# Differences of the Fourier matrix blocks made in layer 1's prologue, beside the value products, and loaded by both Fourier layers

## The chip, the cores and the metric

The kernel runs on one core of one Trainium2 chip. The metric is the device time of one execution in microseconds (us), given as the median over runs. A core has a matrix engine (PE, with its weight loads shown as PEld), a vector engine (DVE), a scalar engine (ACT), a general engine (POOL), and SyncE (SP), whose queue issues nearly all transfers (DMA) here. In the text, layers are counted from 0.

## The reference

Four layers are applied to x of shape 2048 × 640 in float32: sliding-window attention, Fourier mixing, attention, Fourier mixing. Each is added to its input.

```python
def _A_ref(x, wqkv, wo):                       # layers 0 and 2
    H = 32; Dh = D // H; W = 256
    q, k, v = ...                              # x @ wqkv, split into 32 heads of 20
    scores = jnp.einsum("bhqd,bhkd->bhqk", q, k) * (Dh ** -0.5)
    mask = (idx[:, None] - idx[None, :] >= 0) & (idx[:, None] - idx[None, :] < W)
    p = _softmax(jnp.where(mask[None, None], scores, -1e9))
    return (p @ v) @ wo
def _B_ref(x, dft_seq_re, dft_seq_im, dft_hid_re, dft_hid_im):   # layers 1 and 3
    a = jnp.einsum("bsd,ed->bse", x, dft_hid_re)
    b = jnp.einsum("bsd,ed->bse", x, dft_hid_im)
    return jnp.einsum("ts,bse->bte", dft_seq_re, a) - jnp.einsum("ts,bse->bte", dft_seq_im, b)
x = x + _A_ref(_layernorm(x), ...)
x = x + _B_ref(_layernorm(x), ...)
```

and the last two lines once more.

## The kernel before

**Layers.** `network` calls `attention` for layers 0 and 2 and `fourier` for layers 1 and 3. The instructions of each engine run in the order in which the code writes them: the schedule is manual, and where functions are interleaved, a hand-written order with posted work and due times decides. Every product is made of three products of rounded halves: `split` (L223 on; its rows show as L226 on ACT and L232 on DVE) cuts an operand into a high and a low half.

**The Fourier layers' first pass.** The product with the sequence matrix is done in four passes (sb, part), each with eight blocks j of 128 rows. A fast-multiplication scheme with seven products uses, beside the matrix's own blocks, differences of them. The input `c` holds for every (sb, part, j) a row of four blocks of 512 columns, c0 to c3; the scheme needs c1 − c0 (kind 0, units "a1" and "a2"), c2 − c1 (kind 1, units "b", "b7", "b5") and c2 − (c1 − c0) (kind 2, unit "g"). Pass (0, 0) is special: it runs while the attention layer ahead of it is still finishing its last rows (`late`, with `staged` posted into it), so its products (L1415) stand among that layer's output products and hidden-dimension products (L239, L694). `load_to` issues the loads, `cut_to` makes the differences and splits them, `seq` issues the products.

In layer 1, `load_to` fetches 512 KB pieces of c (L1268), `cut_to` and `staged` make the 24 differences (L1287, L1324, L1335 and L1344, on DVE or POOL), and `keep` has each stored to a scratch tensor `c_d` in device memory (256 KB each, issued from `seq`). `sums_kept` is set at the end of the first Fourier layer. In layer 3, `load_to` then fetches the block itself and the stored difference in 256 KB pieces (L1254, L1264, L1266), and the subtractions are left out, but for L1346, which makes a further difference in both layers. The later passes make their differences themselves in both layers.

**The prologue of layer 0.** `before_heads` normalizes x, transposes it, multiplies it by the weights of q, k and v, and ends before the first head. Its tiles t = 0 to 15 have 128 rows each. `prep` loads one tile ahead (L318), takes its statistics on DVE (L286 to L290), normalizes it (L304) and turns it on PE (L341). `value(t)` (a value call) makes two products on PE of 128 × 320 for tile t, 15 matmuls each, in two PSUM banks out of three (5, 6, 7) that the role "v" takes in turn: six banks for three calls, so the first bank of a call is one that the second half of the call two before, or the first half of the one before, had. After the products comes `prep()`, and then the two halves are copied out of PSUM, the first by ACT, the second by DVE (L442). Every second call stores 768 KB of values to `v_d` (L444). Ahead of each of the calls 4 to 7, 8 to 11 and 12 to 15 stand `packed` steps, which issue 24, 12 and 12 transfers `kp<-qk_d` and `qp<-qk_d` of 80 KB (L594) on SP. Between them stand `pieces`, products for q and k (L239 too). After call 15 the first head's projection begins (L257); its banks are two of the same three.

SP issues in the order of the code. A transfer that has to wait for a semaphore (data to store, a buffer to be free) holds back what stands behind it in that queue.

**Buffers.** `pt` is four tiles of 128 × 1536. `pt[0]` and `pt[1]` stage the values in the prologue (in the rows: pt_95, pt_96). `pt[2]` and `pt[3]` (pt_97, pt_98) hold raw value weights at the very start and are then free until the heads.

Of the kernel before, what the change touches and what calls it, by code (L numbers as in the profile page):

```python
# [7 lines left out]
F32 = mybir.dt.float32  # L8
# [56 lines left out]
class Net:  # L65
    def __init__(self, nc, tc, ctx, a):
# [27 lines left out]
        self.rd = dram.tile([NSB, H, 512], F32, name="r_d")  # L94
        self.cd = dram.tile([3, NB // 2, P, 512], F32, name="c_d")
        self.sums_kept = False
        self.xs = [dram.tile([S, D], F32, name=f"x_d{i}") for i in range(3)]
# [270 lines left out]
    def before_heads(self, xsrc):  # L368
# [47 lines left out]
        def pieces(sb):  # L416
            for c in range(2):
# [4 lines left out]
                if ready or sb and state[0] < 4 * sb + 8:  # L422
                    prep()

        def value(t):
            v, xt = vst[t // 2 % 2], self.xnt(t // 4)
            rs = slice((t % 4) * P, (t % 4 + 1) * P)
            ps = []
            for hf in range(2):
# [4 lines left out]
                ps.append(p)  # L434
            prep()
            for hf in range(2):
                dst = v[:, 4 * hf:4 * hf + 4, t % 2, 0:84].rearrange("p q (h c) -> p q h c", c=21)[:, :, :, 1:21]
                src = ps[hf].rearrange("p (q h c) -> p q h c", q=4, h=4)
                if hf == 0:
                    nc.scalar.activation(dst, src, AF.Copy)  # L440
                else:
                    nc.vector.tensor_copy(dst, src)  # L442
# [43 lines left out]
        packed(3)  # L486
        values(3)
        self.ones_rows(1)

# [541 lines left out]
    def late(self, xsrc, xdst, hook):  # L1031
# [30 lines left out]
        for t in range(NB):  # L1062
# [32 lines left out]
            if t == NB - 2:  # L1095
                u = self.last_a2 - 1
                self.post(3, lambda u=u: self.staged(u, 0, nc.vector))
                self.post(6, lambda u=u: self.staged(u, 1))
                self.post(9, lambda u=u: self.staged(u, 2))
            hook(t)  # L1100
# [92 lines left out]
    def take_fourier(self):  # L1193
# [23 lines left out]
        self.acc = {}  # L1217
        self.leaving, self.keeping = [], []

# [28 lines left out]
    def load_to(self, n):  # L1248
        while self.n_load <= min(n, len(self.order) - 1):
# [3 lines left out]
            if ph == "a2" and self.kept_sum(u):  # L1253
                self.nc.sync.dma_start(self.t1[j], self.cd[0, j])  # L1254
            if ph in ("a2", "b5"):
# [17 lines left out]

    def keep(self, u, t):

        sb, part, ph, j = self.order[u]
        if not self.sums_kept and sb + part == 0:
            kind = {"a1": 0, "b": 1, "b7": 1, "g": 2}[ph]
            self.keeping.append(lambda: self.nc.sync.dma_start(self.cd[kind, j], t))

    def staged(self, u, stage, eng=None):
# [10 lines left out]
        self.split(c[0], c[1], (q, p)[stage - 1])  # L1292
        out.append(c)
        if stage == 1:
            self.kept[j] = c

    def cut_to(self, n):
        nc = self.nc
        while self.n_cut <= min(n, len(self.order) - 1):
# [5 lines left out]
            if ph == "b7":  # L1305
                if j:
                    self.staged(u, 0, nc.gpsimd)
                    self.staged(u, 1)
                    self.staged(u, 2)
                continue  # L1310
# [10 lines left out]
            if ph in ("a", "a1"):  # L1321
                eng = nc.vector if ph == "a1" else nc.gpsimd
                if not self.kept_sum(u):
                    eng.tensor_tensor(out=t1, in0=q, in1=p, op=OP.subtract)  # L1324
                    if ph == "a1":
                        self.keep(u, t1)
                src = [p] + ([t1] if ph == "a" else [])
# [5 lines left out]
            elif ph == "b":  # L1333
                if not self.kept_sum(u):
                    nc.vector.tensor_tensor(out=p, in0=q, in1=p, op=OP.subtract)  # L1335
                    self.keep(u, p)
                src = [q, p]
            else:
                cut(q)
                eng = nc.vector if self.order[u][:2] == (0, 0) and j < 3 else nc.gpsimd  # L1340
                if self.kept_sum(u):
                    t1, p = p, t1
                else:
                    eng.tensor_tensor(out=t1, in0=p, in1=t1, op=OP.subtract)  # L1344
                    self.keep(u, t1)
                nc.vector.tensor_tensor(out=p, in0=t1, in1=q, op=OP.subtract)  # L1346
# [227 lines left out]
    def fourier(self, xsrc, xdst, more):  # L1574
# [205 lines left out]
        for g in range(NB // 2):  # L1780
# [11 lines left out]
        self.ready, self.hid, self.sums_kept = 8, False, True  # L1792

# [71 lines left out]
```

## Time and profile before

| | |
|---|---|
| runs | 2188.59, 2188.83, 2190.87 us; median 2188.83 |
| profiled execution, its own time | 2191.25 us |
| its span, first to last instruction | 2189.5 us |
| mean granted PE clock | 0.996 |
| transfers | 398.40 MB, mean 182 GB/s |
| read from and written to device memory | 273.94 and 120.06 MB |
| value calls 4 to 7 in layer 0, on PE | 53.14 to 72.6 us |
| layer 1's first pass beside the attention tail | about 533 to 652 us |
| the same in layer 3 | about 1626 to 1733 us |

Times in the profile count from the first instruction. A row of a timeline has the start, the duration, the engine and line, the operation with its output and inputs, the number of instructions, and in brackets the idle time ahead of it on its engine with what released it. For SP (shown as SPq) the duration is the time from the first issue of a group to the end of its last, waits between them included. The sum of the busy times is far above the span, because engines work side by side; what counts is what the engine that ends last waits for. Three rows of the page's groups and issues belong to the parts that the change touches:

```profile
L1344 POOL TENSOR_TENSOR pt<-pt,pt 128x512 f32<-128x512 f32 x32 | 46.2, 1445 | 232.5 <-DMA pt<-c 146.0
L226 ACT ACTIVATE c<-pt 128x512 fp32r<-128x512 f32 x146 | 90.4, 625 | 108.2 <-POOL pt L1324 56.4
pt<-c SPq DMA_DIRECT2D x166, 512.0 KB
```

The columns of the first two are: busy us and mean ns of one, then the idle time of the engine ahead of the group and what ended it. The third is a group of transfers: loads of c, 166 of them, 512 KB at the median.

### The profile page before, as it was taken

What the parts mean: (1) busy time and instruction counts of PE and PEld (TensorE: products, weight loads), DVE (VectorE), ACT (ScalarE), POOL (GpSimd) and SP (SyncE); (2) the same over time, 40 slices, a digit from 0 to 9 for tenths busy, and PEclk for the clock granted to TensorE, in tenths of its full rate; (3) what the DMA queues carried; (4) which work ended last, traced back from release to release, by engine and by line L of the source; (5) the groups of instructions that cost most, each with busy time, mean ns of one, the idle gap of its engine ahead of it and who ended that gap; (6) DMA issues with size and microseconds to landing.
All of it is one profiled execution on the core that took longest, in us unless ns stands there. A gap on an engine that the chain in (4) does not pass through costs nothing.

```text
span 2189.5 us, 48923 instructions
## 1 busy us (share of the span) xinstructions
PE 2119.5 (97%) x17872; PEld 1785.8 (82%) x17872; DVE 1600.5 (73%) x3931; ACT 1139.8 (52%) x2125; POOL 958.5 (44%) x1562
## 2 busy tenths in 40 slices
PE   7999999898999999999999999998999999999999
PEld 7987777677878888889999877776778888888899
DVE  6358888786897868786661588887867968687766
ACT  3117777656554545452341277776566645455332
POOL 3037776765513232332330376767655023241324
PEclk9999999999999999999999999999999999999999
DMA  5546666785566454656646566667855454546653
GB/s 183 175 156 190 199 180 210 213 222 172 200 192 188 129 183 140 212 185 200 205 156 177 161 187 196 186 204 208 216 165 180 141 187 135 166 152 209 225 166 126
DMA packets 227088, 398.40 MB, mean 182 GB/s; under 512 B 39968, under 2 KB 86560, under 8 KB 226848
## 3 DMA queue, kind: packets, MB, share of 16 engines
q1 hardware_dynamic: 226848, 395.28, 57.8%
q8 instruction: 141, 2.31, 0.5%
q14 instruction: 99, 0.81, 0.1%
HBM read 273.94 MB, written 120.06 MB: 180 GB/s over the span
## 4 chain that ended last, share of the span: by engine, by line
PE 79%; DVE 6%; DMA 4%; ACT 4%; POOL 3%; issue 2%; SPq 1%; ACTq 0%; DVEq 0%; POOLq 0%
PE banks L1415 29%; PE banks L239 15%; PE banks L257 12%; PE banks L694 6%; PE banks L659 5%; PE banks L1703 5%; PE banks L631 5%; DVE banks L636 1%; DMA qp<-qk_d 1%; ACT pt L669 1%; DVE qp L232 1%; PE banks L341 1%; DMA qk_d<-c 1%; ACT big L1038 1%; SPq L594 1%
## 5 line engine op out<-in xcount | busy, mean ns | idle before, releaser
L636 DVE CUSTOM_DVE_ANT_0 banks<-banks,mask 128x384 f32<-128x384 f32 (+2 forms) x1024 | 527.1, 556 | 121.4 <-PE banks L631 98.6
L669 ACT ACTIVATE pt<-banks 128x768 f32<-128x768 f32 (+2 forms) x512 | 393.5, 771 | 170.7 <-PE banks L659 59.8
L675 POOL TENSOR_SCALAR_AFFINE_SELECT pt<-pt 128x256 f32<-128x256 f32 x512 | 213.8, 418 | 220.3 <-ACT pt L669 201.6
L257 PE MATMUL banks<-big,wc 64*128 64x512 f32 x1920 | 271.4, 394 | 0.4 <-DVE pt L442 0.4
L659 PE MATMUL banks<-qp,kp 61*128 61x384 f32 (+2 forms) x1024 | 211.4, 382 | 24.2 <-DVE mc L636 17.0
L631 PE MATMUL banks<-kp,qp 60*128 60x384 f32 (+2 forms) x1024 | 206.9, 348 | 8.8 <-DVE mc L636 8.5
L694 PE MATMUL banks<-pt,vq 128*32 128x128 f32 x5760 | 211.2, 278 | 3.5 <-ACT pt L669 3.5
L257 PEld LDWEIGHTS banks<-big,wc 64*128 64x128 f32 x1920 | 187.3, 186 | 22.2 <-ACT x L544 1.3
L679 POOL TENSOR_SCALAR_AFFINE_SELECT pt<-pt 128x256 f32<-128x256 f32 x448 | 193.8, 433 | 0.0
L226 ACT ACTIVATE qp<-pt 128x512 fp32r<-128x512 f32 (+1 forms) x200 | 123.1, 625 | 129.3 <-DVE pt L1346 50.2
L232 DVE TENSOR_TENSOR qp<-pt,qp 128x512 fp32r<-128x512 f32 (+1 forms) x198 | 156.3, 797 | 40.9 <-ACT qp L226 39.3
L694 PEld LDWEIGHTS banks<-pt,vq 128*32 128x32 f32 x5760 | 142.2, 110 | 51.5 <-issue 36.2
L659 PEld LDWEIGHTS banks<-qp,kp 61*128 61x128 f32 x1024 | 108.6, 185 | 88.8 <-DVE mc L636 65.8
L1415 PE MATMUL banks<-qp,big 128*128 128x512 f32 x648 | 153.6, 391 | 0.1
L631 PEld LDWEIGHTS banks<-kp,qp 60*128 60x128 f32 x1024 | 124.7, 187 | 33.7 <-DVE mc L636 21.8
L1344 POOL TENSOR_TENSOR pt<-pt,pt 128x512 f32<-128x512 f32 x32 | 46.2, 1445 | 232.5 <-DMA pt<-c 146.0
L226 ACT ACTIVATE c<-pt 128x512 fp32r<-128x512 f32 x146 | 90.4, 625 | 108.2 <-POOL pt L1324 56.4
L636 DVE DVE_READ_ACCUMULATOR2_ANT mc<- 128x1 f32 x1024 | 144.3, 141 | 0.0
L1415 PEld LDWEIGHTS banks<-qp,big 128*128 128x128 f32 x648 | 120.8, 188 | 24.9 <-POOL qp L232 0.9
L232 DVE TENSOR_TENSOR c<-pt,c 128x512 fp32r<-128x512 f32 x144 | 116.6, 813 | 26.7 <-ACT c L226 24.1
L1415 PE MATMUL banks<-qp,xc 128*128 128x512 f32 x480 | 118.2, 394 | 3.6 <-DVE xc L232 2.1
L552 POOL CAST c<-x 128x512 fp32r<-128x512 f32 x64 | 38.9, 611 | 166.5 <-ACT x L544 162.3
(253 smaller groups left out, 4477.0 us busy)
## 6 DMA issues: line engine op xcount, KB each, us to landing
pt<-c SPq DMA_DIRECT2D x166, 512.0 KB
qk_d<-c SPq DMA_DIRECT2D x80, 512.0 KB
kp<-qk_d SPq DMA_DIRECT2D x384, 80.0 KB
qp<-qk_d SPq DMA_DIRECT2D x384, 80.0 KB
kp<-u_d SPq DMA_DIRECT2D x32, 640.0 KB
o_d<-ou SPq DMA_DIRECT2D x64, 256.0 KB
x_d<-x SPq DMA_DIRECT2D x48, 320.0 KB
v_d<-pt SPq DMA_DIRECT2D x16, 768.0 KB
```

The costliest lines, as they stand in the source:

```text
L226: nc.scalar.activation(hi, src, AF.Copy, scale=-1.0 if neg else 1.0)
L232: (eng or nc.vector).tensor_tensor(out=lo, in0=src, in1=hi.bitcast(F32), op=OP.subtract)
L239: self.nc.tensor.matmul(p, x, y, start=n == 0, stop=n == last)
L257: self.nc.tensor.matmul(ps[a], x[r], y[r], start=half + i == 0, stop=half == 1 and i == n - 1, skip_group_check=True)
L631: nc.tensor.matmul(p, qp[quad % 2][b:b + 60, z, qb * P:(qb + 1) * P], kp[quad % 2][b:b + 60, z, k0 * P:(qb + 1) * P], start=True, stop=True)
L636: nc.vector.tensor_tensor_reduce(out=p, in0=p, in1=self.mask[:, 384 - n * P:], scale=1.0, scalar=NEG, op0=OP.add, op1=OP.max, accum_out=mc ...
L659: nc.tensor.matmul(self.banks[:, banks[e], :n * P], kp[quad % 2][b:b + 61, z, kb * P:(kb + 1) * P], qp[quad % 2][b:b + 61, z, kb * P:(kb + ...
L669: nc.scalar.activation(pt[quad, kb][:, 2 * z:2 * z + 2, :n * P], self.banks[:, b0:b1 + 1, :n * P], AF.Exp, scale=SCALE)
L675: nc.gpsimd.affine_select(out=t[:, :, 0:P], in_=t[:, :, 0:P], pattern=[[0, 2], [1, P]], compare_op=OP.is_ge, fill=0.0, base=0, channel_mul ...
L679: nc.gpsimd.affine_select(out=t[:, :, 256:384], in_=t[:, :, 256:384], pattern=[[0, 2], [-1, P]], compare_op=OP.is_gt, fill=0.0, base=0, ch ...
L694: nc.tensor.matmul(self.banks[32 * h:32 * h + 32, bank, :P], vq[:, 96 * (kb % 4) + 21 * h:96 * (kb % 4) + 21 * h + 32], t[:, h, (qb - kb) ...
L1415: nc.tensor.matmul(self.banks[:, bk, :], p, b[q], start=start and m == 0, stop=stop and last and m == 2, skip_group_check=True)
```

## The change

A new function `presum(n)` in `before_heads` makes all 24 differences of pass (0, 0), for layer 0 alone (`first`). For each j there are three stages, one per value call: load c0, c1 and c2 (768 KB) into `pt[2]` or `pt[3]`; subtract three times in place on DVE; store the 768 KB to `c_d`, which now has one row of 1536 columns per j. Even j use `pt[2]`, odd j `pt[3]`, one call later. It is called as `presum(t - 4)` in `value(t)`, after the products and `prep()` and ahead of the two copies out of PSUM, and once more after the last call, where it stores j = 7. So call 4 loads j = 0; call 5 subtracts j = 0 and loads j = 1; call 15 stores j = 6 and subtracts j = 7.

Both Fourier layers then load their differences: `kept_sum` is true for every unit of pass (0, 0). `keep`, `keeping` and `sums_kept` are gone, `staged` has lost its subtracting stage, and `posted` work for it at delay 3 too.

```diff
@@ before_heads
+        def presum(n):
+            for b in range(2):
+                j, stage = 2 * ((n - b) // 3) + b, (n - b) % 3
+                if not 0 <= j < NB // 2:
+                    continue
+                t = self.pt[2 + b]
+                c0, c1, c2 = cuts(t, 512)
+                if stage == 0:
+                    nc.sync.dma_start(t, a["c"][0, 0, j][:, :1536])
+                elif stage == 1:
+                    for out, x, y in ((c0, c1, c0), (c1, c2, c1), (c2, c2, c0)):
+                        nc.vector.tensor_tensor(out=out, in0=x, in1=y, op=OP.subtract)
+                else:
+                    nc.sync.dma_start(self.cd[j], t)
...
@@ value
             prep()
+            if first:
+                presum(t - 4)
             for hf in range(2):
...
@@ end of before_heads
         values(3)
+        if first:
+            presum(NB - 4)
...
@@ load_to
             if ph == "a2" and self.kept_sum(u):
-                self.nc.sync.dma_start(self.t1[j], self.cd[0, j])
+                self.nc.sync.dma_start(self.t1[j], self.cd[j, :, :512])
...
                 if ph != "a1":
-                    self.nc.sync.dma_start(p, self.cd[1 + (ph == "g"), j])
+                    at = 1024 if ph == "g" else 512
+                    self.nc.sync.dma_start(p, self.cd[j, :, at:at + 512])
...
     def kept_sum(self, u):
-        return self.sums_kept and self.order[u][:2] == (0, 0)
+        return self.order[u][:2] == (0, 0)
-
-    def keep(self, u, t):
...
@@ staged
-        if stage == 0:
-            if not self.kept_sum(u):
-                eng.tensor_tensor(out=p, in0=q, in1=p, op=OP.subtract)
-                self.keep(u, p)
-            return
...
@@ cut_to
             if ph in ("a", "a1"):
-                eng = nc.vector if ph == "a1" else nc.gpsimd
-                if not self.kept_sum(u):
-                    eng.tensor_tensor(out=t1, in0=q, in1=p, op=OP.subtract)
-                    if ph == "a1":
-                        self.keep(u, t1)
+                if ph == "a":
+                    nc.gpsimd.tensor_tensor(out=t1, in0=q, in1=p, op=OP.subtract)
...
@@ seq
-        for f in self.keeping:
-            f()
-        self.keeping.clear()
```

PE's instructions keep their order. What moves on SP and DVE stands in three places. The first is SP's queue in layer 0's prologue, from the packing before value call 4 to the stores of call 7. Before:

```order
L594 DMA kp_561<-qk_d 20x2x512 x6
L594 DMA qp_106<-qk_d 20x2x512 x6
L318 DMA x<-x 128x640 x2
L444 DMA v_d<-pt_95 128x8x192
L444 DMA v_d<-pt_96 128x8x192
L524 DMA qk_d<-c 128x2x512 x2
```

and with the change:

```order
L613 DMA kp_561<-qk_d 20x2x512 x6
L613 DMA qp_106<-qk_d 20x2x512 x6
L317 DMA x<-x 128x640
L433 DMA pt_97<-c 128x1536
L317 DMA x<-x 128x640
L433 DMA pt_98<-c 128x1536
L461 DMA v_d<-pt_95 128x8x192
L438 DMA c_d<-pt_97 128x1536
L433 DMA pt_97<-c 128x1536
L438 DMA c_d<-pt_98 128x1536
L461 DMA v_d<-pt_96 128x8x192
L543 DMA qk_d<-c 128x2x512 x2
```

Five transfers of 768 KB stand between the tiles of x and the value stores, the first load ahead of the second x tile.

The second place is DVE in the value calls 5 and 6 (a call's rows begin with the split of the turned tile, `big<-banks,big`, and the copies are L442 before and L459 after). Before:

```order
L232 TENSOR_TENSOR big_512<-banks,big_512 128x4x128
L232 TENSOR_TENSOR big_512<-banks,big_512 128x128
L442 COPY pt_95<-banks 128x4x4x20
L286 BN_STATS st<-x 128x6 x2
L288 BN_AGGR mv<-st 128x2
L290 TENSOR_SCALAR rs<-mv 128x1
L304 TENSOR_SCALAR x<-x,mv,rs 128x640
L232 TENSOR_TENSOR big_732<-banks,big_732 128x4x128
L232 TENSOR_TENSOR big_732<-banks,big_732 128x128
L442 COPY pt_96<-banks 128x4x4x20
```

and with the change:

```order
L231 TENSOR_TENSOR big_512<-banks,big_512 128x4x128
L231 TENSOR_TENSOR big_512<-banks,big_512 128x128
L436 TENSOR_TENSOR pt_97<-pt_97 128x512 x3
L459 COPY pt_95<-banks 128x4x4x20
L285 BN_STATS st<-x 128x6 x2
L287 BN_AGGR mv<-st 128x2
L289 TENSOR_SCALAR rs<-mv 128x1
L303 TENSOR_SCALAR x<-x,mv,rs 128x640
L231 TENSOR_TENSOR big_737<-banks,big_737 128x4x128
L231 TENSOR_TENSOR big_737<-banks,big_737 128x128
L436 TENSOR_TENSOR pt_98<-pt_98 128x512 x3
L459 COPY pt_96<-banks 128x4x4x20
```

Three subtractions stand ahead of each copy, behind the splits.

The third place is SP's queue around the value calls 12 to 15, from the packing before them to the first transfers for the heads. Before:

```order
L594 DMA qp_106<-qk_d 20x2x512 x6
L444 DMA v_d<-pt_95 128x8x192
L444 DMA v_d<-pt_96 128x8x192
L492 DMA kp_104<-ones 1x32x128 x2
L621 DMA vq_92<-v_d 128x384
L621 DMA vq_93<-v_d 128x384
```

and with the change:

```order
L613 DMA qp_106<-qk_d 20x2x512 x6
L438 DMA c_d<-pt_97 128x1536
L433 DMA pt_97<-c 128x1536
L438 DMA c_d<-pt_98 128x1536
L461 DMA v_d<-pt_95 128x8x192
L433 DMA pt_98<-c 128x1536
L438 DMA c_d<-pt_97 128x1536
L461 DMA v_d<-pt_96 128x8x192
L438 DMA c_d<-pt_98 128x1536
L511 DMA kp_104<-ones 1x32x128 x2
```

Each load of c into a buffer now stands right behind the store out of the same buffer, or two places behind it.

More of the change, by code (lines that the diff above doesn't have):

```diff
@@ L94, in __init__ @@
         self.rd = dram.tile([NSB, H, 512], F32, name="r_d")
-        self.cd = dram.tile([3, NB // 2, P, 512], F32, name="c_d")
-        self.sums_kept = False
+        self.cd = dram.tile([NB // 2, P, 1536], F32, name="c_d")
         self.xs = [dram.tile([S, D], F32, name=f"x_d{i}") for i in range(3)]
@@ L1096, in late @@
                 u = self.last_a2 - 1
-                self.post(3, lambda u=u: self.staged(u, 0, nc.vector))
-                self.post(6, lambda u=u: self.staged(u, 1))
-                self.post(9, lambda u=u: self.staged(u, 2))
+                self.post(6, lambda u=u: self.staged(u, 0))
+                self.post(9, lambda u=u: self.staged(u, 1))
             hook(t)
@@ L1217, in take_fourier @@
         self.acc = {}
-        self.leaving, self.keeping = [], []
+        self.leaving = []
     def take_rest(self):
@@ L1271, in kept_sum, with staged @@
     def kept_sum(self, u):
-        return self.sums_kept and self.order[u][:2] == (0, 0)
-    def keep(self, u, t):
[L1276 to L1281, printed above, removed]
+        return self.order[u][:2] == (0, 0)
+    def staged(self, u, stage):
         j, out = self.order[u][3], self.cut_of.setdefault(u, [])
         p, q = cuts(self.raw_of[u], 512)
-        if stage == 0:
-            if not self.kept_sum(u):
-                eng.tensor_tensor(out=p, in0=q, in1=p, op=OP.subtract)
-                self.keep(u, p)
-            return
         c = self.ring.popleft()
         self.ring.append(c)
-        self.split(c[0], c[1], (q, p)[stage - 1])
+        self.split(c[0], c[1], (q, p)[stage])
         out.append(c)
-        if stage == 1:
+        if stage == 0:
             self.kept[j] = c
@@ L1306, in cut_to @@
                 if j:
-                    self.staged(u, 0, nc.gpsimd)
+                    self.staged(u, 0)
                     self.staged(u, 1)
-                    self.staged(u, 2)
                 continue
@@ L1335, in cut_to @@
                     nc.vector.tensor_tensor(out=p, in0=q, in1=p, op=OP.subtract)
-                    self.keep(u, p)
                 src = [q, p]
@@ L1339, in cut_to @@
                 cut(q)
-                eng = nc.vector if self.order[u][:2] == (0, 0) and j < 3 else nc.gpsimd
                 if self.kept_sum(u):
@@ L1343, in cut_to @@
                 else:
-                    eng.tensor_tensor(out=t1, in0=p, in1=t1, op=OP.subtract)
-                    self.keep(u, t1)
+                    nc.gpsimd.tensor_tensor(out=t1, in0=p, in1=t1, op=OP.subtract)
                 nc.vector.tensor_tensor(out=p, in0=t1, in1=q, op=OP.subtract)
@@ L1791, in fourier @@
                     behind(at)
-        self.ready, self.hid, self.sums_kept = 8, False, True
+        self.ready, self.hid = 8, False
 def network(nc, tc, a, layers=4):
```

## The prediction

> **What bounds the kernel now.** I read the page's header, busy time and chain of waits first.
>
> ```profile
> span 2189.5 us, 48923 instructions
> PE 2119.5 (97%) x17872; PEld 1785.8 (82%) x17872; DVE 1600.5 (73%) x3931; ACT 1139.8 (52%) x2125; POOL 958.5 (44%) x1562
> PE 79%; DVE 6%; DMA 4%; ACT 4%; POOL 3%; issue 2%; SPq 1%; ACTq 0%; DVEq 0%; POOLq 0%
> ```
>
> TensorE is busy 97% of the span and carries 79% of the chain. The change touches no matrix product, so it can gain only where PE waits for another engine, and loses wherever it makes PE wait. Two places are touched. The first is layer 1's Fourier pass. The view of stretches (start:end, length, then busy of PE, weight loads, DVE, ACT, POOL; granted clock, DMA share, GB/s), cut at the same two PE groups in layers 1 and 3, compares the layer that makes the differences with the one that loads them:
>
> ```profile
> 533.37:651.86 118.49, 109.38 (x545) 89.61 (x544) 103.86 (x236) 67.92 (x139) 42.67 (x48) 0.99 0.62 200
> 1625.91:1733.18 107.27, 104.47 (x545) 89.37 (x545) 90.94 (x219) 67.97 (x139) 37.88 (x45) 1.00 0.56 178
> ```
>
> The same 545 products take 118.49 against 107.27 us: 11.22 us, with DVE 12.92 us busier. The PE timeline (start, duration, group, idle before it) shows where:
>
> ```profile
> 542.27 1.15 PE L239 MATMUL banks<-qp,kp 128*128 128x320 f32 x6 [1.68 <-DVE big L977]
> 569.61 2.02 PE L239 MATMUL banks<-qp,kp 128*128 128x320 f32 x12 [1.75 <-DVE x L1077]
> 642.89 3.79 PE L1415 MATMUL banks<-qp,xc 128*128 128x512 f32 x9 [1.39 <-ACT xc L226]
> ...
> 1658.29 2.02 PE L239 MATMUL banks<-qp,kp 128*128 128x320 f32 x12 [0.64 <-DVE x L1077]
> 1725.02 3.56 PE L1415 MATMUL banks<-qp,xc 128*128 128x512 f32 x15
> ```
>
> Layer 1's waits are for DVE and ACT, and after the one at 642.89 nine products take 3.79 us where fifteen take 3.56 in layer 3.
>
> The second place is the prologue, layer 0 before its heads:
>
> ```profile
> 50.00:75.00 25.00, 23.27 (x157) 22.20 (x155) 14.25 (x40) 4.67 (x13) 3.91 (x5) 1.00 0.69 207
> 100.00:125.00 25.00, 25.00 (x156) 23.81 (x156) 4.11 (x7) 4.29 (x9) 0.00 (x0) 1.00 0.50 158
> ```
>
> DVE is busy 14.25 and 4.11 of 25 us, so there is room on the engine by its average. But PE is full too, so any new wait here adds to the time.
>
> **The change, part by part.**
>
> *Layer 1's pass.* Gone are 24 subtractions (DVE's and some of POOL's) and 24 stores; the 512 KB loads become the 256 KB pieces that layer 3 has. With the same order, layer 1 should run like layer 3, except the wait of 1.68 us at 542.27: it is on the eviction L977 of the attention tail's banks, which stand in another rotation in layer 3 and are not touched. I leave 1.2 of it standing (an estimate: part of a delay of 1.68 is taken back where PE waits next for DVE anyway). Gain 11.22 − 1.2 = 10.0; bounds 8 (if the later loads wait, as the 1.75 at 569.61 partly survives in layer 3 with 0.64) and 11.2.
>
> *The prologue's work.* Eight 768 KB loads, eight 768 KB stores (12.6 MB), 24 subtractions on DVE. DVE rows for that shape and the value copy they are put in front of:
>
> ```profile
> 634.89 0.69 DVE L1344 TENSOR_TENSOR pt<-pt,pt 128x512 f32<-128x512 f32 x1
> 635.61 0.69 DVE L1346 TENSOR_TENSOR pt<-pt,pt 128x512 f32<-128x512 f32 x1
> 64.63 0.48 DVE L442 COPY pt<-banks 128x320 f32<-128x320 f32 x1
> 92.32 0.49 DVE L442 COPY pt<-banks 128x320 f32<-128x320 f32 x1 [3.98 <-PE banks L239]
> 125.54 0.49 DVE L442 COPY pt<-banks 128x320 f32<-128x320 f32 x1 [3.92 <-PE banks L239]
> ```
>
> Three cost 2.1 us at their pitch of 0.72, 24 cost 17. Before its copies DVE idles 3.9 to 4.0 us, which would hide 2.1. What is not hidden is the wait for the load: the subtractions stand on DVE ahead of the copy that empties the second half's bank, and a DVE that waits for c holds that bank. Three banks rotate, two per call: call 7's first half takes the bank that call 5's copy empties, call 11's that of call 9, and the first L257 product that of call 15. Those three PE rows and the queue of SP, which issues in order:
>
> ```profile
> 67.97 1.56 PE L239 MATMUL banks<-kp,big 128*128 128x320 f32 x9
> 74.33 1.13 PE L341 MATMUL banks<-ident,x 128*128 128x128 f32 x5 [1.72 <-DVE x L304]
> 96.45 1.48 PE L239 MATMUL banks<-kp,big 128*128 128x320 f32 x9
> 126.09 2.10 PE L257 MATMUL banks<-big,wc 64*128 64x512 f32 x16 [0.39 <-DVE pt L442]
> ...
> 72.44 0.89 DVE L286 BATCH_NORM_STATS2 st<-x 128x6 f32<-128x320 f32 x2 [7.32 <-DMA x<-x]
> ...
> 67.77 1.28 SPq L318 DMA_DIRECT2D x<-x  x2
> 88.86 3.76 SPq L594 DMA_DIRECT2D qp<-qk_d  x6
> 92.98 9.08 SPq L444 DMA_DIRECT2D v_d<-pt  x2
> 113.44 2.80 SPq L594 DMA_DIRECT2D qp<-qk_d  x6
> 117.30 9.18 SPq L444 DMA_DIRECT2D v_d<-pt  x2
> ```
>
> The transfers' rate comes from slices of 2 us of the DMA view from 50 us:
>
> ```profile
> GB/s 174 253 166 277 141 169 177 151 195 208 240 369 68 0 97 333 225 151 266 153 151 154 321 133 0 0 226 167 249 13 285 251 171 203 301 108 0 0 157 246
> ```
>
> 369 GB/s is the highest: 768 KB take at least 2.1 us there.
>
> *Wait 1, call 7.* SP reaches the load of c0 only behind 24 packing transfers and one x tile, at 68.4. That x tile, issued at 67.77, lands at 72.44. c0 stands behind it on the queue; I add its 2.1 us at the best rate: 74.5. Subtractions to 76.6, copy to 77.1. Call 7 started at 67.97: 9.1 late. PE already loses 1.72 at 74.33 to the same late x tile, which this covers: +7.4. Bounds 5 (c0 abreast of x, at 72.2) and 9 (nothing covered). [...]
>
> *Wait 2, call 11.* c3 stands behind the next 12 packing transfers, at 88.86 + 3.76 = 92.6. What before had in flight from then was those and one 768 KB store:
>
> ```profile
> 93.00:98.00 5.00, 5.00 (x36) 5.00 (x35) 0.49 (x1) 0.44 (x1) 0.00 (x0) 1.00 0.70 213
> 98.00:101.60 3.60, 3.60 (x25) 3.47 (x24) 0.48 (x1) 0.44 (x1) 0.00 (x0) 1.00 0.00 0
> ```
>
> They were through by 98.0. c3 has that store's place: in at 98.2. Subtractions 2.1, copy 0.5: 100.8 against 96.45, +4.4. Bounds 3.2 (in at 97.0) and 7 (the store of c2 abreast of it costs another 2.1 to 2.6).
>
> *Wait 3, the first L257.* Both difference buffers are in use, so c6's load waits on SP for the store of c4, and c7's for that of c5. The store of c4 follows the third packing, 113.44 + 2.80 = 116.2, where before had its value store:
>
> ```profile
> 117.20:121.20 4.00, 4.00 (x30) 4.00 (x29) 0.10 (x2) 0.44 (x1) 0.00 (x0) 1.00 0.77 247
> 121.20:126.00 4.80, 4.49 (x31) 4.16 (x30) 0.88 (x3) 1.16 (x3) 0.00 (x0) 1.00 0.00 0
> ```
>
> Through by 121.2. c6 goes at 121.3, abreast of the store of c5 and the value store; I give it 4.2 us, as the 4.0 of that store with the packing's rest: 125.5. c7 goes when c5's store is in, 127.5, and takes 4.1 likewise: 131.6. Three subtractions to 133.7, copy to 134.1, against 126.09: +8.0. Bounds 5 (both chained transfers at 2.7) and 11 (5.6 each, with three abreast). Queued behind the waiting subtraction on DVE is only the copy (in the calls before, the next tile's statistics too); behind c6's blocked load on SP stand c5's store, the value store and c7's load, then the ones rows and v tiles of the first heads, which need the last value store and so call 15's copy anyway. They shift with PE, and nothing is won back.
>
> *Half clock.* One wait in layer 1 shows what an idle PE costs afterwards:
>
> ```profile
> 643.00:647.70 4.70, 4.57 (x12) 3.31 (x13) 4.67 (x7) 2.92 (x7) 1.83 (x1) 0.64 0.65 194
> ```
>
> After the 1.39 us before 642.89 (and shorter ones ahead) the granted clock is 0.64 over 4.70 us. 36% of that is 1.7 us; nine products at layer 3's pace are 2.14 (9/15 of 3.56), so the first nine alone lose 1.65, and with the edges of the stretch I take 2.1. Waits of 4 to 9 us should do this each time: 3 × 2.1 = 6.4; bounds 0 (the prologue's 1.72 at 74.33 left the clock at 1.00) and 8. The Trainium skill ("TensorE: Matmul & The Clock Gate", Part 1: HAM) has the clock halved after one idle window of about 3.4 us and full again after a busy one: an estimated 1.7 for each wait, 5.1 in place of 6.4. That short waits leave it full agrees with 74.33; that 1.39 us were enough at 642.89 does not, unless the waits ahead of it count.
>
> *Waits between* (calls 8, 12) fall on pairs of products that do not use the banks held. The seven fewer rows on DVE and the larger stores elsewhere cost nothing that PE waits for.
>
> **Sum:** 7.4 + 4.4 + 8.0 + 6.4 = +26.2; − 10.0 = +16.2. The profiled span goes from 2189.5 to 2205.7. That execution took 2191.25 in all, 1.75 around its span and 2.4 over the median of the runs, 2188.83; the median goes to 2205. Lower end 5 + 3.2 + 5 + 3 − 11.2 = +5 (half clock at 3, since not all three waits will be short); upper 9 + 7 + 11 + 8 − 8 = +27.
>
> **Rivals.**
>
> *The loads come a call early (faster).* If c lands while DVE is idle anyway, the subtractions take only the 3.9 us gaps, and nothing is added: −10, 2179. For it: DVE's 4.11 of 25 us, and the rate falls to 0 at 98.00. Against: the SP rows, which put every load behind packing transfers. It decides where c0 lands before 65.4, three subtractions and a copy ahead of call 7's start; SP cannot issue it by then.
>
> *Only the first wait is paid.* The DMA idles in 98.00:101.60 and 121.20:126.00; if later loads slip into such gaps, what is left is 7.4 + 2.1 − 10 = −0.5: 2188. Against: the loads' issue follows the packing, and the gap comes after.
>
> *The prologue is bound by transfers.* 12.6 MB at 369 GB/s are 34 us if nothing overlaps; − 10 = +24, 2213. For it: a DMA share of 0.69 in 50.00:75.00. Against: 0.50 in 100.00:125.00.
>
> *Layer 1 does not speed up,* because its 256 KB differences land late behind the attention tail's stores: the full 26, 2215. Against: layer 3 loads the same pieces at 0.56 of the DMA.
>
> **How the numbers follow.** The sum has 0.70, the early loads 0.06, only the first wait 0.08, the transfer bound 0.10, no gain 0.06. A measurement of this kernel can tell about 0.2% (4.4 us) from no change. Of the first-wait case I count 0.04 as slower, 0.03 as same and 0.01 as faster; the early loads are faster; the rest slower: 0.07, 0.03, 0.90. The likeliest case's own range is 2194 to 2216, the sum's bounds. The range, 2190 to 2218, adds the no-gain case and a margin towards the first-wait case for waits that fall under their bounds.
>
> **What would show it.** Right: PE rows of about 9, 4 and 8 us of idle before call 7, call 11 and the first L257, released by the DVE copy, with DVE itself waiting for c's DMA ahead of the subtractions; a granted clock under 1 right behind each; layer 1's stretch at 107 to 110 us, its dip at 643 gone. Wrong: no such idle with the prologue's length unchanged (the early loads), waits in all calls with the DMA share near 1 (the transfer bound), or layer 1's stretch still near 118.

## The result, and the profile after

| | us |
|---|---|
| before, median of 4 runs | 2188.71 (2186.26 to 2190.87) |
| the change, median of 4 runs | 2211.31 (2209.72 to 2211.87) |
| ratio of the runs, 95% interval | 1.0099 (1.0087 to 1.0112); the two medians alone give 1.0103 |
| span of the profiled execution | 2189.5 before, 2208.0 after |

The kernel became 22.6 us slower; 2205 was forecast, in a range from 2190 to 2218. The spans differ by 18.5 us; of the other 4.1, 2.5 is that the profile of before lies above its median (2191.25 against 2188.71) and 1.6 that the profile of after lies below its own (2209.72 against 2211.31).

The chain of waits of the page after:

```profile
PE 76%; DVE 7%; DMA 7%; ACT 4%; issue 3%; POOL 3%; SPq 1%; ACTq 0%; DVEq 0%; POOLq 0%
```

PE has fallen from 79% to 76% of the chain, and transfers rose from 4% to 7%. The stretches of layer 0's prologue, in the columns of the prediction's (start:end, length, PE, PEld, DVE, ACT, POOL, granted clock, DMA share, GB/s):

```profile
50.00:75.00 25.00, 18.50 (x124) 17.64 (x122) 12.03 (x32) 4.95 (x14) 3.13 (x4) 0.93 0.71 220
75.00:100.00 25.00, 22.78 (x128) 21.44 (x129) 15.88 (x34) 4.48 (x11) 1.56 (x2) 0.86 0.76 252
100.00:125.00 25.00, 21.76 (x122) 20.31 (x121) 8.31 (x14) 3.14 (x6) 0.00 (x0) 0.93 0.78 258
125.00:151.00 26.00, 14.83 (x102) 14.50 (x100) 7.14 (x13) 2.03 (x5) 0.00 (x0) 0.85 0.79 256
```

PE was full in 100:125 before; it now lacks 2 to 11 us of each stretch, and the clock is under 1 in all four. The PE timeline names the places (call 7, call 8, call 11, call 12, the first L257 of before, which is L256 here, and the first head's second row of scores):

```profile
77.22 2.77 PE L238 MATMUL banks<-kp,big 128*128 128x320 f32 x9 [8.72 <-DVE pt L459]
...
92.28 1.56 PE L238 MATMUL banks<-kp,big 128*128 128x320 f32 x9
...
108.96 2.52 PE L238 MATMUL banks<-kp,big 128*128 128x320 f32 x9 [3.24 <-DVE pt L459]
...
121.82 1.48 PE L238 MATMUL banks<-kp,big 128*128 128x320 f32 x9
...
151.02 3.78 PE L256 MATMUL banks<-big,wc 64*128 64x512 f32 x16 [11.19 <-DVE pt L459]
190.79 0.44 PE L678 MATMUL banks<-qp,kp 61*128 61x384 f32 x1 [0.29 <-DVE mc L655]
```

The same rows before, beside those that the prediction shows:

```profile
83.18 1.56 PE L239 MATMUL banks<-kp,big 128*128 128x320 f32 x9
107.68 1.48 PE L239 MATMUL banks<-kp,big 128*128 128x320 f32 x9
163.08 0.44 PE L659 MATMUL banks<-qp,kp 61*128 61x384 f32 x1 [0.28 <-DVE mc L636]
```

The difference of each pair is how late PE is by then: 9.25 at call 7, 9.1 at call 8, 12.5 at call 11, 14.1 at call 12, 24.9 at L257 and 27.7 in the first head. It stays there through all the heads: at the row where layer 1's stretch begins it is 27.2 (560.54 against 533.37). Each wait is released by DVE's copy L459, and DVE's timeline shows what held that copy:

```profile
74.62 2.14 DVE L436 TENSOR_TENSOR pt<-pt 128x512 f32<-128x512 f32 x3 [9.62 <-DMA pt<-c]
106.36 2.14 DVE L436 TENSOR_TENSOR pt<-pt 128x512 f32<-128x512 f32 x3 [8.91 <-DMA pt<-c]
...
141.04 2.14 DVE L436 TENSOR_TENSOR pt<-pt 128x512 f32<-128x512 f32 x3 [9.66 <-DMA pt<-c]
...
148.43 2.14 DVE L436 TENSOR_TENSOR pt<-pt 128x512 f32<-128x512 f32 x3 [4.84 <-DMA pt<-c]
```

c0, c3, c6 and c7 are waited for, and the copy stands behind. In layer 1 the other half of the forecast shows, in the stretch with the same two PE groups as its ends, and in its PE rows:

```profile
560.54:668.93 108.39, 104.55 (x544) 89.29 (x544) 91.30 (x219) 67.82 (x139) 37.42 (x45) 1.00 0.55 176
```

```profile
569.16 1.15 PE L238 MATMUL banks<-qp,kp 128*128 128x320 f32 x6 [1.40 <-DVE big L996]
593.91 2.02 PE L238 MATMUL banks<-qp,kp 128*128 128x320 f32 x12 [0.64 <-DVE x L1096]
...
660.77 3.56 PE L1412 MATMUL banks<-qp,xc 128*128 128x512 f32 x15
```

108.39 in place of 118.49 us: 10.1 gained. The wait on the eviction that the change does not touch stayed (1.40), the 1.75 went to layer 3's 0.64, and the fifteen products behind the old dip take 3.56, as in layer 3. What is left to the span's 18.5 came later: PE is 17.1 us late behind layer 1's stretch (668.93 against 651.86), and 1.4 more are lost after it in this execution.

### The profile page after: what moved, and what is told of

Same layout as the page of the kernel before. It is cut to its first block, busy times and chain, and to the rows that moved or that the text cites. A ratio compares the mean times of both kernels' runs of the same rounds, so it can differ in the third digit from the quotient of the medians.

```text
span 2208.0 us, 48957 instructions
## 1 busy us (share of the span) xinstructions
PE 2123.3 (96%) x17872; PEld 1792.8 (81%) x17872; DVE 1600.0 (72%) x3937; ACT 1140.3 (52%) x2125; POOL 949.6 (43%) x1556
## 4 chain that ended last, share of the span: by engine, by line
PE 76%; DVE 7%; DMA 7%; ACT 4%; issue 3%; POOL 3%; SPq 1%; ACTq 0%; DVEq 0%; POOLq 0%
PE banks L1412 29%; PE banks L256 13%; PE banks L238 12%; PE banks L713 7%; PE banks L678 6%; PE banks L650 5%; PE banks L1700 4%; DMA kp<-u_d 1%; DVE banks L655 1%; DMA qk_d<-c 1%; DMA pt<-c 1%; ACT pt L688 1%; POOL rs L1105 1%; DMA kp<-qk_d 1%; PE banks L340 1%
## 5 line engine op out<-in xcount | busy, mean ns | idle before, releaser
L256 PE MATMUL banks<-big,wc 64*128 64x512 f32 x1920 | 273.8, 397 | 11.2 <-DVE pt L459 11.2
L256 PEld LDWEIGHTS banks<-big,wc 64*128 64x128 f32 x1920 | 189.1, 188 | 33.4 <-DVE pt L459 11.3
```

The costliest lines, as they stand in the source:

```text
L256: self.nc.tensor.matmul(ps[a], x[r], y[r], start=half + i == 0, stop=half == 1 and i == n - 1, skip_group_check=True)
```

## The experiments

Theory A is the prediction's: a subtraction that waits on DVE for c holds the bank that its call's copy would empty, and PE waits for the bank. Theory B, its rival, has the mass of the transfers make everything in the prologue late; theory C, the work of the subtractions itself. Every time is a median beside runs of the kernel before on the same chip; the ratio is to those, with its 95% interval. "Late" is again the start of a PE row less its start before.

**Subtractions behind the copies.** The three subtractions are kept in a list until the call's copies out of PSUM are issued.

```diff
-                    for out, x, y in (...):
-                        nc.vector.tensor_tensor(out=out, in0=x, in1=y, op=OP.subtract)
+                    todo.append(subtract)
...
                     nc.vector.tensor_copy(dst, src)
+            while todo:
+                todo.pop()()
```

> Each call's three subtractions stand behind its copy out of PSUM; transfers keep their places. Theory A (a subtraction that waits for c holds the bank that its call's copy would empty): the 8.7 us ahead of call 7 and the 3.2 us ahead of call 11 go; what remains is that later work on DVE stands behind the waiting subtraction: the x tile of the next turn (about 4 more us at the first transposes after call 7), call 15's copy behind the wait for c6 (2 to 3 us) and the first masks of the heads behind that for c7 (4 to 6 us). With layer 1's gain of 10 the time is 2190 to 2200. Theory B (12.6 MB more transfers make everything in the prologue late): the time stays within 3 us of the change's, 2208 to 2214.

2200.08 us (2198.37 to 2207.28) against 2188.80; ratio 1.0056 (1.0039 to 1.0073). The PE waits in its prologue:

```profile
77.81 1.33 PE L340 MATMUL banks<-ident,x 128*128 128x128 f32 x5 [5.66 <-DVE x L303]
140.13 3.78 PE L256 MATMUL banks<-big,wc 64*128 64x512 f32 x16 [8.49 <-DVE pt L463]
```

The waits ahead of calls 7 and 11 are gone, and the later work on DVE is late in the two places that were named: the x tile (5.66, where before had 1.72) and call 15's copy, which stands behind the wait for c6. That second wait is 8.49, not 2 to 3. So the bank held by a waiting subtraction is shown as the cause of the first two waits, but 2200.08 is at, and by a hair past, the outermost end of what theory A allowed: something else makes c6 late. Its load is issued only at 132.24, though PE no longer waits ahead of calls 7 and 11.

**Transfers without subtractions.** c itself is stored where the differences belong.

```diff
                 elif stage == 1:
-                    for out, x, y in (...):
-                        nc.vector.tensor_tensor(out=out, in0=x, in1=y, op=OP.subtract)
+                    pass
```

> All loads and stores of the prologue, without the 24 subtractions (c itself is stored in the place of the differences). Theory A: nothing on DVE waits for c, so PE's three long waits go although the transfers stay; 2179 to 2184, that is before less 10 with up to 5 us for x tiles and values that come later. Theory B: at least half of the prologue's 27 us stays, 2192 or more.

2189.89 us (2187.84 to 2193.57) against 2188.80; ratio 1.0007 (0.9996 to 1.0018). Between the two theories: neither range held. PE's rows:

```profile
126.29 2.12 PE L256 MATMUL banks<-big,wc 64*128 64x512 f32 x16 [0.40 <-DVE pt L458]
...
154.32 0.69 PE L649 MATMUL banks<-kp,qp 60*128 60x384 f32 x2 [6.70 <-ACT mt L665]
```

All value calls are as punctual as before (126.09), although every transfer is there: the transfers alone do not make the prologue's products late. But the wait has moved into the first head. The timeline there, SP's and ACT's rows:

```profile
144.38 0.32 SPq L437 DMA_DIRECT2D c_d<-pt  x1
...
149.06 0.43 SPq L518 DMA_DIRECT2D x<-wqk  x1
...
153.28 0.83 ACT L218 ACTIVATE wc<-x 128x384 fp32r<-128x384 f32 x2 [10.74 <-DMA x<-wqk]
```

The next chunk of weights is issued at 149.06, behind the last store to c_d at 144.38; in before it was issued at 130.99. ACT waits for it, and PE for ACT. This wait was in none of the prediction's parts; in the change it lies hidden under the 11 us ahead of L256.

**The same without c6 and c7.** Again without subtractions, the loads and stores of j = 6 and 7 are left out too, and the layers load pieces of c in their place.

```diff
-                if not 0 <= j < NB // 2:
+                if not 0 <= j < 6:
```

> As the run without subtractions, and also without the loads and stores of c6 and c7 (c is stored in the place of the differences, and for j = 6 and 7 the layers load pieces of c of the same size). If the 6.7 us that the first head's scores waited there come from SP's queue, where its weights stood behind the last loads and stores, they and the half clock behind them go, and 8 to 9 of the 12 us over the run without presum with them: 2179 to 2183 against 2189.9. If it is the mass of all transfers of the prologue, 2186 or more.

2179.68 us (2175.90 to 2185.39) against 2190.10; ratio 0.9949 (0.9931 to 0.9967). The wait in the first head is gone, and the time is where the queue's order was forecast to put it. But a quarter of the transfers went together with the last loads and stores, and around that wait, from 145 to 154 us, the run before had the DMA's share at 1.01. So this run does not part the queue's order from the mass of bytes.

**Subtractions without loads.** Old contents of the two buffers are subtracted and stored; POOL sets the part of them that nothing has written to 1 ahead of the prologue.

```diff
                 if stage == 0:
-                    nc.sync.dma_start(t, a["c"][0, 0, j][:, :1536])
+                    pass
```

> The 24 subtractions and eight stores in their places, without the loads of c (old contents of the buffers are subtracted and stored). Theory A: the subtractions find their data ready and fit into DVE's idle time of 3.9 us ahead of each copy; 2178 to 2182. Theory C (DVE's own 17 us of work ahead of the copies make PE late): 2185 or more.

2183.16 us (2177.55 to 2187.88) against 2188.80; ratio 0.9974 (0.9962 to 0.9986). Just outside theory A's 2182. Its profile has PE 2.2 us late at L256 (128.32 against 126.09) with no long wait: 24 subtractions and eight stores with their data at hand cost the prologue some 2 us, not 27. Its span (2186.1) is 10.8 us above that of the next run's trace (2175.3): 3.0 of them are there at L256, 5.0 more come by the end of layer 1's pass, the rest later. Why the 5.0 and the rest come stays open.

**Layer 1 alone.** No `presum`; the Fourier layers load pieces of c of the same size instead of the differences.

```diff
-            if first:
-                presum(t - 4)
...
-                self.nc.sync.dma_start(self.t1[j], self.cd[j, :, :512])
+                self.nc.sync.dma_start(self.t1[j], self.a["c"][0, 0, j][:, :512])
```

> No presum at all; the Fourier layers load pieces of c of the same size in place of the stored differences. Theory A: the prologue is as before, and layer 1's stretch as in the change (108.4 against 118.5 us): 2178 to 2180 against 2188.7. If part of layer 1's 10.1 us came from its later start or another state behind the prologue, more than 2182.

2176.55 us (2172.57 to 2182.60) against 2188.80; ratio 0.9946 (0.9929 to 0.9964), a gain of 8 to 15 us, and 1.5 us below the 2178 to 2180 expected. In its trace the stretch of layer 1 has the change's length: the rows that stand at 569.16 and 660.77 in the change are at 540.03 and 631.64 here, 91.61 us apart in both. The layer's gain is its own and needs nothing of the prologue; what is above 10 us of this run's gain arises outside that stretch.

**c0 and c1 loaded early.** In the change, these two loads alone move ahead of the 24 packing transfers.

```diff
+        if first:
+            for j in range(2):
+                nc.sync.dma_start(self.pt[2 + j], a["c"][0, 0, j][:, :1536])
         self.take_qk("kp", 0)
...
                 if stage == 0:
-                    nc.sync.dma_start(t, a["c"][0, 0, j][:, :1536])
+                    if j > 1:
+                        nc.sync.dma_start(t, a["c"][0, 0, j][:, :1536])
```

> The change, with the loads of c0 and c1 alone moved ahead of the 24 packing transfers in front of value call 4. Theory A (wait 1 is c0's place on the queue): c0 is in before call 5's subtractions, so the 8.7 us ahead of call 7 and the half clock behind it (about 2.4) go, but the last x tiles come 1 to 4 us later; 2201 to 2207 against 2211.3. If the wait is of the transfers' mass, not the place: 2209 or more.

2206.20 us (2203.16 to 2211.23) against 2189.17; ratio 1.0079 (1.0065 to 1.0094). Its PE waits:

```profile
78.12 1.33 PE L340 MATMUL banks<-ident,x 128*128 128x128 f32 x5 [5.57 <-DVE x L303]
105.82 1.59 PE L238 MATMUL banks<-kp,big 128*128 128x320 f32 x9 [2.97 <-DVE pt L460]
147.42 3.78 PE L256 MATMUL banks<-big,wc 64*128 64x512 f32 x16 [12.26 <-DVE pt L460]
```

The wait ahead of call 7 is gone, and the x tile behind the two loads takes most of its place. Call 11 starts 3.1 us earlier than in the change (105.82 against 108.96), and L256 3.6 earlier.

**PE kept busy through the waits.** Products whose results are not used stand ahead of calls 7 and 11 and of the first L256, to see what the half clock costs. In the first of two runs 26, 9 and 34 of them:

```diff
+            if first and t in (7, 11):
+                busy({7: 26, 11: 9}[t])
...
             presum(NB - 4)
+            busy(34)
```

> The change with 26, 9 and 34 more products of 128x320 on PE (their results are not used) ahead of value calls 7 and 11 and of the first L257, which fill the three waits to some 0.7 us. If the half clock behind the waits costs 6 to 7 of the prologue's 27 us, as the granted clock has it: 2203 to 2206 against 2211.3. If the clock's dips cost nothing: 2210 to 2213.

2209.58 us (2207.43 to 2220.29) against 2190.10; ratio 1.0092 (1.0072 to 1.0112). That lies between the two cases and decides nothing: the 309 ns that one product takes were taken for their pitch, but one starts 0.15 us behind the other, so 4.36, 2.95 and 5.79 us of the three waits stayed. The second run has 52, 26 and 68:

> The run that keeps PE busy, with 52, 26 and 68 products: one starts 0.15 us after the other, so the 26, 9 and 34 of before filled only half of the waits (4.36, 2.95 and 5.79 us stayed idle, and the clock fell to 0.81, 0.60 and 0.73 behind them). Now about 1 us of each should stay. If the half clock behind the waits costs what the granted clock has (7.1 us in the change): no dip, 2203 to 2206. If PE makes up for it, or something else sets the pace behind the waits: 2208 or more.

2208.24 us (2205.46 to 2214.11) against 2188.77; ratio 1.0100 (1.0077 to 1.0123). The time alone does not decide: it lies at the edge of the second case, and the distance of the medians to before is 19.5 us, against 22.6 in the change. Its PE rows and two of its stretches:

```profile
76.05 1.58 PE L238 MATMUL banks<-kp,big 128*128 128x320 f32 x9 [0.62 <-DVE pt L466]
107.48 1.58 PE L238 MATMUL banks<-kp,big 128*128 128x320 f32 x9 [1.25 <-DVE pt L466]
118.80 1.48 PE L238 MATMUL banks<-kp,big 128*128 128x320 f32 x9
150.93 3.78 PE L256 MATMUL banks<-big,wc 64*128 64x512 f32 x16 [4.14 <-DVE pt L466]
```

```profile
77.00:84.00 7.00, 7.00 (x44) 6.49 (x43) 6.75 (x17) 1.09 (x3) 1.57 (x2) 1.00 0.82 248
109.00:115.00 6.00, 6.00 (x36) 5.46 (x35) 0.00 (x0) 0.44 (x1) 0.00 (x0) 1.00 0.99 322
```

In the change the same stretches have a clock of 0.65 and 0.72:

```profile
77.00:84.00 7.00, 6.78 (x32) 6.77 (x33) 6.69 (x17) 0.00 (x0) 1.25 (x2) 0.65 0.64 227
109.00:115.00 6.00, 6.00 (x31) 6.00 (x32) 0.30 (x1) 0.44 (x1) 0.00 (x0) 0.72 0.85 269
```

So the first two dips come from the idle PE: they go when it is busy, and call 12 then starts at 118.80, 3.0 us earlier than the change's 121.82. Yet the first L256 starts at 150.93, against 151.02. Nothing of the 3 us arrives there in this trace: something else sets the pace. SP's rows of the change say what:

```profile
110.05 1.11 SPq L438 DMA_DIRECT2D c_d<-pt  x1
117.65 0.33 SPq L433 DMA_DIRECT2D pt<-c  x1
...
119.97 3.81 SPq L543 DMA_DIRECT2D qk_d<-c  x2
...
126.09 2.33 SPq L613 DMA_DIRECT2D kp<-qk_d  x6
...
131.07 0.35 SPq L438 DMA_DIRECT2D c_d<-pt  x1
135.96 0.36 SPq L433 DMA_DIRECT2D pt<-c  x1
136.42 0.37 SPq L438 DMA_DIRECT2D c_d<-pt  x1
...
143.04 0.33 SPq L433 DMA_DIRECT2D pt<-c  x1
```

and of this run:

```profile
108.57 1.11 SPq L438 DMA_DIRECT2D c_d<-pt  x1
117.81 0.33 SPq L433 DMA_DIRECT2D pt<-c  x1
...
119.15 1.61 SPq L551 DMA_DIRECT2D qk_d<-c  x2
...
126.24 2.27 SPq L621 DMA_DIRECT2D kp<-qk_d  x6
```

The load of c5 waits on SP for the store of c3 to land. That store went 1.5 us earlier in this run and landed no earlier; why is open, but the DMA's share was 0.99 in 109.00:115.00. Next come the stores of q and k (qk_d), and then the packing, which loads what they store and so waits until they have landed. In the change the second of the two stores is held until DVE has split the products behind call 11 (DVE's row is at 122.70). With PE early both are out by 120.76, and the packing still starts no earlier, at 126.24 against 126.09. Around it the transfers run at their full rate. Their rate in the change, in 40 slices of 1.25 us from 100 us on:

```profile
GB/s 174 197 226 364 428 265 5 25 329 204 352 383 418 177 39 147 295 342 376 405 410 380 173 157 208 208 406 231 10 74 182 310 393 383 372 252 172 334 428 246
```

From 121.25 to 127.50 it is 342 to 410 GB/s, near the highest of the row, 428. So two paths end together at the packing, one through PE and one through the transfers, and making PE earlier gains nothing. From there on the queue runs as in the change: packing, store of c4 (at 130.90 against 131.07), load of c6, store of c5, load of c7, each pair on one buffer, so each load waits for a store. PE was early and waited for that chain.

**Three subtractions of layer 1 on POOL.** The kernel before, with no `presum`:

```diff
-                eng = nc.vector if self.order[u][:2] == (0, 0) and j < 3 else nc.gpsimd
+                eng = nc.vector if self.order[u][:2] == (0, 0) and j < 0 else nc.gpsimd
```

> The kernel before, with the three g differences of j = 0 to 2 that layer 1 makes on DVE given to POOL, and nothing in the prologue. If DVE's load is what PE waits for in layer 1, some of the 5 us around 642.89 come: 2184 to 2187. If the g difference's own time is (1.4 us on POOL against 0.7 on DVE): 2188 to 2191.

2188.92 us (2186.80 to 2195.74) against 2190.10; ratio 0.9998 (0.9987 to 1.0010). Moving this work off DVE gains nothing; it has to leave the layer, or at least not go to POOL there.

**Four blocks, six blocks.** These two make the differences of j = 0 to 3 (0 to 5) in the prologue, and those of the other j in layer 1 as before. A pair is loaded while the DMA has a gap, is subtracted behind the copies of two later calls, and stored one call after that. With four:

```diff
         values(1)
+        load_pair(0)
         pieces(2)
...
         values(2)
+        load_pair(2)
         pieces(3)
...
+        subs, stores = {8: 0, 9: 1, 12: 2, 13: 3}, {9: 0, 10: 1, 13: 2, 14: 3}
...
     def kept_sum(self, u):
-        return self.sums_kept and self.order[u][:2] == (0, 0)
+        return self.order[u][:2] == (0, 0) and (self.sums_kept or self.order[u][3] < self.early)
```

> Differences of j = 0 to 3 alone made in the prologue: loads in pairs where before's queue is idle (behind value calls 7 and 11), subtractions behind the copies of calls 8, 9, 12 and 13, stores one call later; j = 4 to 7 made and stored in layer 1 as before. With a pair ready before its subtractions and 6.3 MB in place of 12.6, the prologue should lose 0 to 3 us; of layer 1's 10 us those around the last unit's first blocks (the stretch behind 642.89, j = 0 to 2, 4 to 6 us) should come: 2183 to 2187, faster than before by 2 to 6 us. If transfers of any size here delay the heads, 2190 or more.

2183.87 us (2180.26 to 2188.38) against 2189.17; ratio 0.9980 (0.9969 to 0.9990). Faster than the kernel before, by about 5 us, and so than the change. The first L257, the nine products of layer 1's dip, and two stretches of the prologue:

```profile
125.02 2.11 PE L257 MATMUL banks<-big,wc 64*128 64x512 f32 x16 [0.40 <-DVE pt L451]
...
636.27 2.75 PE L1431 MATMUL banks<-qp,xc 128*128 128x512 f32 x9 [0.67 <-ACT xc L226]
```

```profile
75.00:100.00 25.00, 25.00 (x159) 23.74 (x158) 11.18 (x23) 4.29 (x11) 0.78 (x1) 1.00 0.82 270
100.00:125.00 25.00, 24.62 (x152) 23.12 (x150) 8.61 (x15) 4.29 (x9) 0.00 (x0) 1.00 0.92 292
```

The prologue loses nothing (125.02 against 126.09), with PE busy 25.00 and 24.62 of 25 us at a clock of 1.00 while the DMA is busier (0.82, 0.92) than in the change (0.76, 0.78). This run has half the bytes, other places for the loads, and the copies first, and does not say which of the three does it. In layer 1 the nine products of the old dip take 2.75 in place of 3.79, behind a wait of 0.67 in place of 1.39.

With six, the third pair is loaded ahead of the first packing and subtracted behind the copies of calls 4 and 5:

> As the run of four, with a third pair loaded ahead of the first packing (subtracted behind the copies of calls 4 and 5): j = 0 to 5. The prologue loses 1 to 6 us (the last x tiles behind two more loads), layer 1 gains 7 to 9: 2181 to 2188.

2188.69 us (2185.42 to 2192.82) against 2189.17; ratio 0.9996 (0.9987 to 1.0006), just above the 2181 to 2188 expected. The early pair puts 5.31 us of wait ahead of the transposes of the last x tiles, as in the run with early loads, and that eats the gain.

## Why the prediction was right, point by point

| step | forecast, us | measured, us |
|---|---|---|
| wait 1 and the half clock behind it | 7.4 + 2.1 | 9.1 (at call 8) |
| wait 2, call 11 | 4.4 | 3.4 (12.5 − 9.1) |
| half clock behind it | 2.1 | 1.6 (14.1 − 12.5) |
| wait 3, first L257 | 8.0 | 10.8 (24.9 − 14.1) |
| half clock behind it | 2.1 | 2.8 (27.7 − 24.9) |
| layer 1 | −10.0 | −10.1 |
| sum, against the span | +16.2 | +17.6, and 18.5 with what came later |

*Direction, places and releaser* were right: the three waits stand at the calls that the banks' rotation gave, all released by the copy L459 behind a subtraction that waits for c. The run with the copies first takes the first two away, and the run without subtractions all three.

*Wait 1* was right to half a microsecond: c0 was in when the subtractions began, at 74.62, where the prediction had 74.5, and PE was 9.25 late at call 7, where it had 9.1. That c0's place on the queue makes it is shown by the run with early loads, with the limit that the x tile then takes its place.

*Wait 3 was mis-sized.* The step had 4.1 us from the store of c4 to the load of c6, 6.2 from there to the load of c7, with the store of c5 between them, and 4.1 from there to the subtractions of c7. In the trace these are 4.9 (131.07 to 135.96), 7.1 (to 143.04) and 5.4 (to 148.43). That is 3.0 longer together, about the 2.8 that were missing.

*Adding the terms up was wrong as a picture,* and that the total came near was luck in part. The sum treated three waits and three half clocks as independent (and took 3 × 2.1 for 6.4). The run that kept PE busy removes the first two dips and starts call 12 3.0 us sooner, and L257 does not start sooner: its time is set by SP's chain of stores and loads into two buffers, which the prediction priced for wait 3 alone and let shift with PE. The run without subtractions agrees: PE is punctual there, and SP still issues the load of c7 at 139.11, only 3.9 us before the change. The rival "bound by transfers" had a part of this. It fell by its own signs, since the waits are not in all calls and the DMA's share is 0.71 to 0.79, but stretches of the chain run at the full rate. The bytes alone do not make L257 late: without subtractions, the same bytes leave it punctual. How much of the chain's length is the queue's order with two buffers, and how much the bytes, no run parts. What the half clock is worth was therefore, by that trace, not 6.4 but what lies behind wait 3, 2.8 us by the rows above; the first two were absorbed, so their rows in the table say how late PE was and not what leaving them out would gain.

*What stood behind the value stores on SP* was named (ones rows, v tiles), and it was said that they shift with PE. The chunk of weights behind them was overlooked. In the run without subtractions it cost PE 6.7 us and a dip (a clock of 0.68 from 154 to 160 us).

*Layer 1's 10.0* was right by the comparison with layer 3, down to the wait that stays and the dip that goes. The rival that it does not come fell with 108.39 us, and the run of layer 1 alone shows the gain to be its own.

*The rival "early loads"* fell with the rows of SP: the first load of c was issued at 68.11. *"Only the first wait"* fell with the waits of 3.24 and 11.19 us at 108.96 and 151.02.

## What to carry to other kernels

Work that waits for a transfer must not stand, on an in-order engine, ahead of an instruction that frees a bank or a buffer for the bound engine: behind the copies the kernel lost 11 us in place of 22, and with its data at hand the same work cost the prologue some 2 us. A layer that runs twice in one kernel, once with and once without some work, prices that work better than a sum of durations. Before waits are added up, look whether a later one is set by a chain that does not pass through the earlier ones: then the longer of the two paths counts, and filling the early gaps can gain nothing, as it did at L257 here.

## What the runs showed of the hardware

A busy DMA need not cost PE anything: in the run of four, at shares of 0.82 and 0.92 over 25 us each (270 and 292 GB/s), PE was busy 25.00 and 24.62 us at a granted clock of 1.00. And the granted clock follows PE's own activity: products with unused results, which filled the waits to 0.62 and 1.25 us, kept it at 1.00 where it had fallen to 0.65 and 0.72 behind waits of 8.72 and 3.24. The Trainium skill ("TensorE: Matmul & The Clock Gate", Part 1: HAM) has the clock at half after an idle window of about 3.4 us and full again after as long a busy one; the dips agree with that in kind, with 35% of 7.00 us (2.4) and 28% of 6.00 us (1.7) lost where its figures make an estimated 1.7 each. The wait of 3.24 is a little shorter than that window and brought a dip all the same.
